# A scan and a gated FFN on one core: the second sequence's decays by matmul, its norm roots kept on chip, and a new order of steps

## The chip, the cores and the metric

The kernel runs on one core of a Trainium2 chip. Five engines work beside each other, each with its own queue that it works off in order: TensorE (PE, with its weight loads shown as PEld), VectorE (DVE), ScalarE (ACT), GpSimd (POOL) and SyncE (SP), which here issues nearly all DMAs. The metric is the device time of one execution in microseconds, as a median over runs. A profiled execution shows every instruction; its span goes from the first to the last instruction.

## The reference

Two blocks follow each other. The first is a state-space scan over 4 sequences with 8 heads, 768 positions, head size 32 and state size 16:

```python
for c in range(nc):                       # chunks of 32
    cum = np.cumsum(log_a[:, :, sl], axis=-1)
    L = np.exp(cum[:, :, :, None] - cum[:, :, None, :]) * causal
    y_intra = ((Cc @ Bc.T) * L) @ xc      # per batch and head
    y_inter = (Cc @ state) * np.exp(cum)[..., None]
    y[:, :, sl] = y_intra + y_inter
    state = decay_full * state + sum_j(B_j x_j * decay_from_j)
```

Its output, as 3072 tokens of 256 numbers, goes through an FFN (d_ff = 1536):

```python
rms = np.sqrt(np.mean(x * x, axis=-1, keepdims=True) + 1e-06)
xn = x / rms * rms_g
return (silu(xn @ w_gate) * (xn @ w_val)) @ w_out
```

## The kernel before

**Sequences.** The scan of a sequence b is cut into six chunks of 128 positions, taken in three pairs (p = 3b, 3b+1, 3b+2). The first two pairs of sequence 0 work on whole chunks, all other pairs on half chunks of 64. For a pair the kernel loads B, C (`bc`) and x, transposes B and C on PE (`turn`, copied out by `T` and `Tt`, and with a decay by `Td`), forms the new states (`A` on PE, `S` on DVE), the products of C and B (`g`), multiplies them by the decay table L (`L`, `L.0`, `L.1.3` and so on, on DVE), and forms the outputs (`y`). A group of A or g products holds both banks of PSUM that single tiles share.

**The decay table L** is made in one of two ways. Sequence 0 sums logs on PE: `log4` takes logs on ACT, `r` multiplies them with a triangular matrix, `parts` splits the result into three bfloat16 parts (`three_parts`), `mask` writes a mask of -2^100 into a pair of banks through an identity (line 445), `sums` adds the row and column sums with small matmuls (lines 459 and 466), and `exp` (line 474) takes the exponential on ACT. Sequences 1 to 3 instead store the sums of logs to DRAM (`rowout`, line 1158), read each row back spread over 64 partitions (`spread`, line 480, two DMAs a chunk), subtract the token's own sum on DVE (`sub`, line 486), take Exp on ACT and put zeros above the diagonal on POOL (`ex`, lines 492 and 494).

**The norm.** `sq` squares y on ACT and adds two halves on POOL, `ms` averages over channels by a matmul with 1/256, `rs` takes (mean + eps)^-1/2 as Exp(-0.5 Ln), and `xn` multiplies it in (line 840). Sequence 0 has the mean on all 128 partitions and uses the roots at once, in a piece of 512 tokens and one of 256 (`ms.0.1`, `rs.0.1`, `xn.0.1`). Sequences 1 to 3 keep the means in four groups of 32 partitions, store the roots to DRAM (line 821) and read them back spread, in four DMAs (`rb`, line 826).

**The FFN.** The weights arrive as 64-bit numbers and are turned into float32 by `pow` (three passes on ACT), `man` and `wt` (DVE). The first half of d_ff for sequence 0 runs early in plain form (`early`, `gate`, `silu`, `hid`, then `late`, `lsilu`, `lhid` for the last 256 tokens; lines 885, 858, 866). After that come stages s0 to s7: sequences 0 to 3 with the first half of the hidden units (s0 has only the output product), then 0 to 3 with the second half. A stage uses products of combined operands: `V` and `U` are combinations on DVE or POOL (a p behind the name means POOL), `P` the gate and value products (line 980), `take` and `C` move and combine them, `silu` and `hid` form the hidden units, `s`, `s2` to `s4` combine these, and `O` are the output products (line 1067).

**The order.** All queues are filled from one written list of about 1,660 steps, in its order. A step reads `0:kind.numbers`, `b1:kind.numbers` or `s1:kind.numbers`, and `/0` to `/2` names the pair of banks of a product in the first part. In front of an activation whose function isn't in the loaded table, the program gets a table load; steps named `table`, `exps` and `set` load one ahead of time.

Of the kernel before, what the change touches and what calls it, by code (L numbers as in the profile page):

```python
# [20 lines left out]
def kernel(  # L21
# [71 lines left out]
    st = {}  # L93

# [230 lines left out]
    def logs_again(g, n):  # L325
        b, c = divmod(g, NC)
        nc.scalar.activation(
            out=la4[g // 4][:, g % 4:g % 4 + n],
            in_=la0[:, c:c + n, b * NH:(b + 1) * NH].unsqueeze(2).to_broadcast([P, n, 4, NH]),
            func=AF.Ln)  # L330

    def minus_mid():
# [5 lines left out]
        "set": lambda: nc.scalar.preload_act_table_set("natural_log_exp_and_others"),  # L338
# [62 lines left out]
    def other_decays():  # L401
        nc.scalar.activation(out=d_sb, in_=ps.pop("d"), func=AF.Exp)
# [87 lines left out]
    def exponential(g):  # L490
        L = pair_tile(g)
        nc.scalar.activation(out=L, in_=L, func=AF.Exp)  # L492
# [300 lines left out]

    def norm_sums(b, third=None):

        if b == 0:
# [12 lines left out]
    def norm_roots(b, third=None):  # L809
        n = TB // 4  # L810
        if third:
            ps["r third"] = r = scan.tile([P, 256], FP32, tag="rest", name="r3", bufs=1)
        elif b == 0:
            ps["r", b] = r = hold.tile([P, 512], FP32, tag="sq2", name="r", bufs=1)
        else:
            r = scan.tile([P, n], FP32, tag="r_sb", name="r4", bufs=2)
        nc.scalar.activation(out=r, in_=ps.pop(("m", b, third)), func=AF.Ln, bias=eps)
        nc.scalar.activation(out=r, in_=r, func=AF.Exp, scale=-0.5)
        if b:
# [50 lines left out]
    def silu_late(f):  # L870
        us["late", f] = hold.tile([P, 256], FP32, tag="u", name="u", bufs=2)
        nc.scalar.activation(out=us["late", f], in_=ps["late", f][:, 0:256], func=AF.Silu)
# [25 lines left out]
    def silu_of(f):  # L898
        if f not in us:
            us[f] = hold.tile([P, 512], FP32, tag="b2", name="u", bufs=NB2)  # L900
            nc.scalar.activation(out=us[f], in_=ps["gv", f][:, 0], func=AF.Silu)
        else:
            nc.scalar.activation(out=us[f], in_=us[f], func=AF.Silu)
# [96 lines left out]
    def silu_gv(n, c, t):  # L1000
# [3 lines left out]
        else:  # L1004
            src = cs[c, n, t]
            u = src[:, half[0]]
        nc.scalar.activation(out=u, in_=src[:, half[0]], func=AF.Silu)  # L1007
# [153 lines left out]
    def row_decays(k):  # L1161
        c = 2 * k
        r_sb = scan.tile([P, P], FP32, tag="r_sb", name="e_sb", bufs=2)
        nc.scalar.activation(out=r_sb, in_=ps["row", k][:, 1], func=AF.Exp)
# [15 lines left out]
    def by_vector(out, in_, scale):  # L1180
# [32 lines left out]
        "table": lambda k: ac.preload_act_table(AF.Silu), "switch": switch,  # L1213
        "exps": lambda: ac.preload_act_table_set("natural_log_exp_and_others"),
# [29 lines left out]
    for name, fn in (("U", combine_u), ("V", combine_v), ("join", joined_gv), ("hid", hide_gv),  # L1244
                     ("two", combine_wo), ("s", combine_h), ("s3", difference_h), ("s2", second_h),
                     ("s4", fourth_h)):
        kinds[name], kinds[name + "p"] = on(dv, fn), on(pl, fn)
    scan_kinds = {
        "turn": of_pair(turn), "T": of_pair(lambda p: turned(p, ac.copy)),
# [10 lines left out]
        "table": lambda b: ac.preload_act_table(AF.Silu),  # L1260
        "exps": lambda b: ac.preload_act_table_set("natural_log_exp_and_others"),
# [3 lines left out]
        0:never 0:after 0:mid 0:fetch.0 0:upto2 0:mids 0:ident16 0:idle.7 0:fetch.1 0:whole16  # L1265
        0:mask.0.0/0 0:whole 0:hmask 0:tmask 0:part 0:gcol 0:part2 0:sel 0:mask.1.1/2 0:after2 0:aT
        0:kinks 0:la0 0:mask.0.1/1 0:log4.0.4 0:fetch.5 0:r.0 0:eps 0:parts.0 0:log 0:d 0:log4.4.2
        0:dx 0:c*2 0:cx 0:scale.0 0:log4.6.2 0:turn.0.1 0:bc.2 0:T.0.1 0:Tt.0.0.1 0:sums.0.1
        0:Tt.0.1.1 0:exp.0.1 0:turn.0.0 0:Tt.0.1.0 0:T.0.0 0:last.0 0:Tl.0 0:cc 0:fetch.3 0:pow.1
        0:sums.0.0 0:A.0 0:sums.1.1 0:man.0 0:fetch.2 0:Tt.0.0.0 0:exp.0.0 0:g.0.1/1 0:x.2 0:fetch.6  # L1270
        0:S.0 0:turn.1.1 0:T.1.1 0:Tt.1.1.1 0:fetch.4 0:middles b1:exps b1:bc.2 0:Tt.1.0.1
        0:turn.1.0 0:Tt.1.1.0 0:T.1.0 0:g.0.0/0 0:man.1 0:tok 0:L.0.1 0:Tt.1.0.0 0:mask.1.0/1
        0:scale.1 0:pow.0 0:man.5 0:tokout 0:row.1 0:rowout.1 0:sums.1.0 0:rowe.1 0:fetch.7
        0:exp.1.1 0:L.0.0 0:last.1 0:man.3 0:wt.0 0:r.1 0:man.2 0:parts.1 0:exp.1.0 0:dT.2 0:g.1.0/2
        0:L.1.0 0:y.0/1 0:Tl.1 0:fetch.11 0:pow.3 0:wt.3 0:g.1.1/0 0:L.1.1 0:A.1 0:S.1 0:wt.1
        0:y.1/2 0:row.0 0:pow.2 0:wt.2 0:sq.0 0:scale.2 0:pow.5 0:turn.2 0:never16 0:yt.0
# [7 lines left out]
        0:L1.2.2 0:L1.2.3 s0:U.1.0 0:L.2.0 0:silu.1 0:hid.1 b1:x.2 0:man.11 0:gate.5/0 0:silu.5  # L1284
        0:hid.5 b1:scale.1 0:fetch.10 0:y.2/2 0:sq.2 b1:bc.0 0:yt.2 b1:scale.0 s0:U.0.0 0:man.10
        0:fetch.9 b1:scale.2 0:man.9 0:ms.0.1 b1:table 0:rs.0.1 0:xn.0.1 0:gate.4/1 b1:dT.1 b1:A.0
        0:silu.4 b2:table b1:x.1 b1:spread.4 b1:spread.5 b1:sub.5 b1:A.1 b1:A.2 0:hid.4 0:ydone.0
        0:ydone.1 0:switch.1 0:pow.10 0:switch.0 0:late.3 0:lsilu.3 b1:S.0 b1:S.1 0:pow.9 b1:S.2
        0:fetch.13 0:late.1 0:lsilu.1 b1:turn.1 b1:Td.1 0:lhid.1 b1:turn.0 b1:Td.0 0:fetch.14
        0:late.0 b1:T.1 b1:Tt.1.1 b1:sub.4 b1:T.0 b1:Tt.0.0 b2:dT.1 b1:Tt.0.1 b1:dT.2 b1:Tt.1.0  # L1290
        0:wt.8 0:wt.9 s0:U.0.3 s0:Up.0.1 b2:bc.1 0:wt.11 b1:ex.4 b1:g.0 b1:L.0.3 s0:U.1.13 0:lhid.3
        b1:L.0.2 b1:turn.2 b1:ex.5 b1:T.2 b1:Td.2 b1:Tt.2.0 0:late.2 b1:L.0 s0:U.1.8 b1:Tt.2.1
        b1:g.1 b1:L.1 0:lsilu.2 b1:L.1.3 0:lsilu.0 b1:L.1.2 b1:y.0.0 b1:y.0.1 s0:U.1.14 b1:y.0.2
        b1:y.1.0 0:lhid.2 0:pow.13 0:lhid.0 0:late.4 0:pow.14 0:fetch.12 0:lsilu.4 s0:s.1 0:pow.12
        s0:Up.0.4 0:wt.10 b2:bc.2 b2:scale.1 s0:Up.1.22 s0:Up.1.3 b2:bc.0 s0:s.0 s0:two.0 0:man.12
        b2:scale.0 b1:y.1.1 b1:y.1.2 b1:y.2.0 b1:y.2.1 b1:y.2.2 0:late.5 b2:x.1 b2:spread.0
        b2:spread.3 b1:sq b2:spread.1 s0:two.1 b1:yt 0:man.13 s0:O.5.0 s0:two.2 0:wt.13 0:wt.12
        s0:O.1.0 s0:U.0.13 b2:spread.2 s0:two.3 b2:x.0 0:lhid.4 0:lsilu.5 b1:ms b1:rs s0:O.1.1
        s0:s3.0 s0:O.4.0 0:lhid.5 s0:s.2 s0:O.1.2 s0:Otake.1 s0:s2.0 0:man.14 b2:scale.2 0:wt.14
        s0:s3.1 s0:O.5.1 s0:s2.1 s0:O.5.2 s0:s2.2 s0:O.4.1 b2:sub.0 s0:O.6.0 s0:s4.0 s0:O.2.0  # L1300
        b2:sub.2 b2:sub.1 s0:O.2.1 s0:U.0.14 s0:O.6.1 s0:O.6.2 s0:s4.1 s0:s3.2 0:fetch.15 s0:O.4.2
        s0:s4.2 b1:rb b1:xn s1:Vp.12 s1:V.0 s0:O.2.2 s0:Oadd.11 s1:Vp.14 b2:x.2 s1:V.1 s0:Otake.6
        s0:O.7.0 s0:O.7.1 s0:O.7.2 s0:Otake.7 s0:Oadd.22 s1:P.13.1 s1:take.13.1 0:pow.15 b2:A.0
        b2:A.1 s1:V.7 s1:V.4 s1:Vp.11 s1:V.8 b2:A.2 s1:P.13.0 s1:Vp.10 s0:O.3.0 b2:spread.4 s0:O.3.1
        s0:O.3.2 b2:ex.0 b2:S.0 b2:S.1 s1:take.13.0 s1:P.11.1 0:fetch.18 b2:sub.3 0:man.15
        s0:Oadd.12 s1:take.11.1 s1:P.11.0 s1:take.11.0 s1:P.4.1 b2:spread.5 b2:sub.5 b2:ex.2 s1:Vp.6
        b2:dT.0 b2:S.2 s1:Vp.3 s1:Vp.9 b2:ex.1 b2:ex.3 s1:P.14.0 s1:take.14.0 s1:P.4.0 s0:Oadd.21
# [183 lines left out]
```

## Time and profile before

| what | us |
|---|---|
| median of 3 runs (434.02 to 437.09) | 434.12 |
| the profiled execution | 435.05 |
| its span, first to last instruction | 433.3 |
| first product of s1 starts (s1:P.13.1) | 111.01 |
| first product of s2 starts (s2:P.13.0) | 167.82 |
| first product of s3 starts (s3:P.13.1) | 219.16 |
| mean granted clock of PE | 0.966 |
| table loads on ACT, each | 1.28 |

Times in the profile count from the start of the span. A row of waits gives an engine and line, what released it, the total, how often, and the longest. A row of the chain gives the start, the time spent, and what the chain went through. A row of the timeline gives start and length, engine, line, operation, what it writes and reads, sizes and how many were merged.

### The profile page before, as it was taken

What the parts mean: (1) busy time and instruction counts of PE and PEld (TensorE: products, weight loads), DVE (VectorE), ACT (ScalarE), POOL (GpSimd) and SP (SyncE); (2) the same over time, 40 slices, a digit from 0 to 9 for tenths busy, and PEclk for the clock granted to TensorE, in tenths of its full rate; (3) what the DMA queues carried; (4) which work ended last, traced back from release to release, by engine and by line L of the source; (5) the groups of instructions that cost most, each with busy time, mean ns of one, the idle gap of its engine ahead of it and who ended that gap; (6) DMA issues with size and microseconds to landing.
All of it is one profiled execution on the core that took longest, in us unless ns stands there. A gap on an engine that the chain in (4) does not pass through costs nothing.

```text
span 433.3 us, 9717 instructions
## 1 busy us (share of the span) xinstructions
PE 402.3 (93%) x3865; PEld 338.1 (78%) x3865; DVE 322.1 (74%) x659; ACT 220.4 (51%) x425; POOL 162.8 (38%) x198
## 2 busy tenths in 40 slices
PE   8889787899798698999999999999999999999996
PEld 5566345579686588887888889898998999998895
DVE  6698878697887678985885796579477737865793
ACT  3788759692399574795624433344134323322310
POOL 3113600520486050293462463637231425442330
PEclk9699798899899989999999999999999999999999
DMA  9784974869419658030450010000102110201112
GB/s 113 174 204 161 184 148 126 140 134 219 116 39 107 194 143 166 26 135 3 129 210 2 0 74 2 1 39 36 37 1 72 39 38 0 75 36 38 36 46 101
DMA packets 96756, 38.37 MB, mean 89 GB/s; under 512 B 77608, under 2 KB 86696, under 8 KB 96712
## 3 DMA queue, kind: packets, MB, share of 16 engines
q1 hardware_dynamic: 92552, 37.50, 36.1%
q10 hardware_dynamic: 4160, 0.26, 0.7%
q8 instruction: 30, 0.49, 0.5%
q14 instruction: 14, 0.11, 0.1%
HBM read 28.54 MB, written 9.21 MB: 87 GB/s over the span
## 4 chain that ended last, share of the span: by engine, by line
PE 69%; ACT 11%; DMA 7%; DVE 5%; issue 3%; SPq 2%; POOL 1%; DVEq 0%; POOLq 0%; ACTq 0%
PE gate L980 33%; PE o L1067 21%; PE val L980 7%; PE y L723 3%; DMA r<-roots 2%; PE g L587 1%; PE gate L858 1%; DMA L<-rowd 1%; ACT p L985 1%; DMA roots<-r 1%; DMA rowd<-r_sb 1%; ACT L1260 1%; DMA wr<-in_moe_w_val_dram 1%; SPq L110 1%; DVE L L627 1%
## 5 line engine op out<-in xcount | busy, mean ns | idle before, releaser
L980 PE MATMUL gate<-V,u 128*128 128x256 f32 x336 | 84.9, 387 | 0.0
L980 PEld LDWEIGHTS gate<-V,u 128*128 128x128 f32 x336 | 61.0, 191 | 9.8 <-ACT p L985 0.7
L1007 ACT ACTIVATE p<-p 128x256 f32<-128x256 f32 x70 | 27.7, 412 | 47.7 <-DVE p L998 47.5
L980 PE MATMUL gate<-xn,u 128*128 128x256 f32 x168 | 44.2, 397 | 5.2 <-DVE xn L840 4.8
L985 ACT COPY p<-gate 128x512 f32<-128x512 f32 x42 | 24.3, 588 | 39.6 <-PE gate L980 36.4
L980 PE MATMUL gate<-V,wgv 128*128 128x256 f32 x168 | 42.6, 384 | 0.5 <-DVE c L998 0.5
L998 DVE TENSOR_TENSOR p<-gate,p 128x512 f32<-128x512 f32 x42 | 28.8, 687 | 16.4 <-PE gate L980 16.1
L980 PEld LDWEIGHTS gate<-xn,u 128*128 128x128 f32 x168 | 31.3, 198 | 11.1 <-DVE xn L840 3.7
L1067 PE MATMUL o<-wo,h 128*128 128x128 f32 x288 | 38.1, 277 | 0.3 <-DVE h L1013 0.3
L1067 PEld LDWEIGHTS o<-wo,h 128*128 128x128 f32 x288 | 36.5, 192 | 2.0 <-DVE h L1013 0.5
L1067 PE MATMUL o<-two,h 128*128 128x128 f32 x288 | 37.3, 275 | 0.0
L1067 PEld LDWEIGHTS o<-two,h 128*128 128x128 f32 x288 | 35.8, 192 | 1.2 <-DVE v L1098 0.2
L1067 PE MATMUL o<-two,s 128*128 128x128 f32 x288 | 36.1, 276 | 0.7 <-ACT xn L790 0.7
L985 ACT COPY p<-val 128x512 f32<-128x512 f32 x42 | 24.2, 584 | 24.1 <-PE val L980 20.7
L1067 PEld LDWEIGHTS o<-two,s 128*128 128x128 f32 x288 | 34.9, 192 | 1.8 <-ACT xn L790 1.1
L980 PEld LDWEIGHTS gate<-V,wgv 128*128 128x128 f32 x168 | 29.9, 190 | 5.6 <-DVE c L998 1.1
L494 POOL TENSOR_SCALAR_AFFINE_SELECT L<-L 64x512 f32<-64x512 f32 x36 | 26.8, 744 | 19.8 <-ACT L L492 18.2
L1013 POOL TENSOR_TENSOR h<-p 128x256 f32<-128x256 f32 x26 | 19.9, 772 | 36.2 <-ACT p L1007 35.3
L1007 ACT ACTIVATE c<-c 128x256 f32<-128x256 f32 x42 | 16.9, 414 | 30.8 <-DVE c L998 30.6
L980 PE MATMUL val<-V,u 128*128 128x256 f32 x112 | 28.5, 380 | 0.0
L998 DVE TENSOR_TENSOR p<-p,gate 128x512 f32<-128x512 f32 x28 | 18.9, 684 | 11.3 <-PE gate L980 8.6
L1013 POOL TENSOR_TENSOR h<-c 128x256 f32<-128x256 f32 x17 | 12.8, 759 | 35.2 <-ACT c L1007 35.2
(215 smaller groups left out, 812.8 us busy)
## 6 DMA issues: line engine op xcount, KB each, us to landing
L<-rowd SPq DMA_DIRECT2D x36, 128.0 KB, 3.4
xr<-in_x_dram SPq DMA_DIRECT2D x24, 128.0 KB, 4.4
wr<-in_moe_w_out_dram SPq DMA_DIRECT2D x6, 512.0 KB
part<-ob SPq DMA_DIRECT2D x8, 384.0 KB, 2.3
before<-part SPq DMA_DIRECT2D x8, 384.0 KB, 3.6
out_dram<-ob SPq DMA_DIRECT2D x8, 384.0 KB
wr<-in_moe_w_val_dram SPq DMA_DIRECT2D x5, 512.0 KB, 4.1
wr<-in_moe_w_gate_dram SPq DMA_DIRECT2D x5, 512.0 KB, 5.4
```

Source lines behind the costliest of these rows:

```text
L110: queue.dma_start(out=st[p]["x"][:, i], in_=x[b, :, sl, :].rearrange("h s n -> s h n"))
L494: nc.gpsimd.affine_select(out=L[r], in_=L[r], pattern=[[0, NH], [1, HC]], compare_op=ALU.is_ge, fill=0.0, base=0, channel_multiplier=-1)
L587: nc.tensor.matmul(out=g[u, P * i:P * i + P].rearrange("p (t m) -> p t m", t=2), lhsT=T[r, i, 0, u], rhs=T[r, i, 1:3, u], start=(first and ...
L627: nc.vector.tensor_tensor(out=L, in0=g.rearrange("p q (i m) -> p q i m", i=2), in1=L, op=ALU.mult)
L723: nc.tensor.matmul(out=y[2 * k + u][rows, (2 * n + i) * HC:(2 * n + i + 1) * HC], start=(k, u, rows.start) not in opened, stop=True, skip_ ...
L858: nc.tensor.matmul(out=gv[:, k], lhsT=w[:, t, fs], rhs=xns[0][:, t, 0:512], start=(t == 0), stop=(t == 1))
L980: nc.tensor.matmul(out=dst[:, half[w]], lhsT=lhsT[:, w], rhs=rhs, start=(k in (13, 14) and w == 0), stop=True, skip_group_check=True)
L985: nc.scalar.copy(out=v, in_=(Xs if chain[k] == "X" else Zs)[n, t])
L998: nc.vector.tensor_tensor(out=o, in0=in0, in1=in1, op=ALU.subtract)
L1007: nc.scalar.activation(out=u, in_=src[:, half[0]], func=AF.Silu)
L1013: engine.tensor_tensor(out=hidden_tile(n, f // 2)[:, f % 2, c % 10 - 1], in0=u, in1=src[:, half[1]], op=ALU.mult)
L1067: nc.tensor.matmul(out=o[:, t * P:(t + 1) * P], lhsT=lhsT[:, t], rhs=rhs, start=(opens and t == 0), stop=True, skip_group_check=True)
```

## The change

Sequence 1 makes its decay table as sequence 0 does: the steps `mask`, `sums` and `exp` exist for its three pairs, with the pair of banks 2, and six `spread`, `sub` and `ex` steps leave the list. For that a third group of log sums is formed (`log4.8.4`, `r.2`, `parts.2`). Sequence 1's roots are made as sequence 0's are, in two pieces on all partitions, and its `rb` step leaves the list. Table loads are made by a helper that remembers the loaded table. The list is in another order from its beginning up to the first product of s3; behind that it is the same.

```diff
+    loaded = [None]
+
+    def table(name):
+
+        if loaded[0] != name:
+            loaded[0] = name
+            if name == "silu":
+                nc.scalar.preload_act_table(AF.Silu)
+            else:
+                nc.scalar.preload_act_table_set("natural_log_exp_and_others")
...
     def logs_again(g, n):
         b, c = divmod(g, NC)
+        if g // 4 == len(la4):
+            la4.append(scan.tile([P, 4, 4, NH], FP32, tag="r_sb", name="la4", bufs=2))
+        table("exp")
         nc.scalar.activation(
...
+        table("exp")
         nc.scalar.activation(out=L.rearrange("p i h m -> p i (h m)"), in_=e, func=AF.Exp)
...
+    WIDE = (0, 1)
+
     def norm_sums(b, third=None):
 
-        if b == 0:
+        if b in WIDE:
             tk = slice(512, TB) if third else slice(0, 512)
...
-        if third:
+        if third and b == 0:
             ps["r third"] = r = scan.tile([P, 256], FP32, tag="rest", name="r3", bufs=1)
         elif b == 0:
             ps["r", b] = r = hold.tile([P, 512], FP32, tag="sq2", name="r", bufs=1)
+        elif b in WIDE:
+            if not third:
+                ps["r", b] = hold.tile([P, TB], FP32, tag="sq2", name="r", bufs=1)
+            r = ps["r", b][:, 512:TB] if third else ps["r", b][:, 0:512]
         else:
             r = scan.tile([P, n], FP32, tag="r_sb", name="r4", bufs=2)
+        table("exp")
         nc.scalar.activation(out=r, in_=ps.pop(("m", b, third)), func=AF.Ln, bias=eps)
+        table("exp")
         nc.scalar.activation(out=r, in_=r, func=AF.Exp, scale=-0.5)
-        if b:
+        if b not in WIDE:
             roots[b] = dram.tile([4, 32, n], FP32, name="roots%d" % b)
...
+    def start_decays_of(p):
+        ps["e", p] = e = pair_of_banks("e", 2)
+        mask(p, e)
+
     scan_kinds = {
+        "mask": of_pair(start_decays_of), "sums": of_pair(lambda p: sums(p, 0, ps["e", p])),
+        "exp": of_pair(lambda p: decay(p, 0, ps.pop(("e", p)))),
...
-        "table": lambda b: ac.preload_act_table(AF.Silu),
-        "exps": lambda b: ac.preload_act_table_set("natural_log_exp_and_others"),
+        "table": lambda b: table("silu"),
+        "exps": lambda b: table("exp"),
...
+        0:scale.2 0:wt.4 b1:x.1 0:T.2 0:ms.0 0:Td.2 0:man.6 0:rs.0 0:xn.0 b1:mask.1 b1:sums.1
+        b1:exp.1 0:pow.5 0:early.1.0/1 0:early.0.1 0:norm.0 0:early.1.1 0:Tt.2.1 0:tok 0:norm.1
+        0:Tt.2.0 b1:mask.0 0:tokout 0:A.2 0:S.2 0:pow.7 b1:sums.0 0:U b1:exp.0 0:gg.2/1 0:L1.2.3
+        0:pow.10 0:wt.5 0:gate.2/0 b1:bc.1 0:wt.6 0:L.2.0 0:L1.2.2 0:man.10 0:pow.8 0:man.7 0:y.2/2
...
+        s0:Up.0.3 0:hid.0 b1:A.0 b1:A.1 b1:dT.2 0:silu.5 0:hid.5 b1:A.2 b1:S.0 s0:Up.0.13 b1:mask.2
+        b1:sums.2 b1:exp.2 b1:S.1 0:ydone.1 0:ydone.0 0:switch.1 0:switch.0 b1:S.2 b2:bc.1 0:late.2
+        0:pow.11 b1:table s0:U.1.0 s0:Up.1.3 b1:g.0 b1:L.0.3 b1:L.0 b1:turn.2 b1:T.2 0:fetch.13
...
+        0:lsilu.5 b2:table s0:O.4.0 b1:ms b1:rs b1:ms.1 s0:O.5.1 b1:rs.1 0:lhid.5 s0:s.2 b2:scale.0
+        s0:twop.2 s0:s2.1 b1:xn 0:man.15 s0:O.2.0 s0:O.2.1 s0:O.2.2 s0:s2p.0 b2:spread.1 s0:O.5.2
+        s1:V.6 s0:U.1.14 0:fetch.14 s0:O.1.0 s0:O.1.1 s0:O.1.2 s0:Otake.1 s1:V.1 s1:Vp.7 s1:P.13.1
```

The helper is called in the same way ahead of the other activations (`exponential`, `row_decays`, `silu_of`, `silu_late`, `silu_gv` and the rest); no line of those functions changes otherwise. In the list before, the same places read:

```diff
-        0:early.0.0/0 0:sq.1 0:rowe.0 0:rowout.0 0:ms.0 0:early.1.0/1 0:wt.5 0:man.6 b1:spread.0
-        b1:spread.2 0:pow.4 0:pow.6 0:T.2 0:man.4 0:rs.0 0:yt.1 0:pow.7 0:man.7 b1:spread.1
-        0:mask.2/2 0:wt.6 0:wt.4 0:early.0.1 0:sums.2 0:xn.0 0:norm.0 0:U 0:wt.7 s0:U.0.8 s0:Up.0.22
-        s0:Up.0.5 b1:sub.0 s0:U.1.5 s0:Up.0.12 b1:dT.0 b1:sub.1 0:exp.2 0:early.1.1 b1:sub.2
-        0:pow.11 b1:ex.0 0:Td.2 s0:Up.1.12 b1:ex.1 s0:Up.0.7 b1:ex.2 b1:spread.3 b1:sub.3 0:Tt.2.0
-        s0:Up.1.7 0:norm.1 0:gate.2/0 b1:ex.3 0:silu.2 0:fetch.8 0:man.8 0:hid.2 s0:U.1.4 0:Tt.2.1
-        0:gate.3/2 0:A.2 0:S.2 0:pow.8 0:silu.3 0:hid.3 0:silu.0 b1:bc.1 b1:x.0 0:hid.0 0:gg.2/1
...
-        s0:s3.0 s0:O.4.0 0:lhid.5 s0:s.2 s0:O.1.2 s0:Otake.1 s0:s2.0 0:man.14 b2:scale.2 0:wt.14
...
-        s0:s4.2 b1:rb b1:xn s1:Vp.12 s1:V.0 s0:O.2.2 s0:Oadd.11 s1:Vp.14 b2:x.2 s1:V.1 s0:Otake.6
```

More of the change, by code (lines that the diff above doesn't have):

```diff
@@ L1006, in silu_gv @@
             u = src[:, half[0]]
+        table("silu")
         nc.scalar.activation(out=u, in_=src[:, half[0]], func=AF.Silu)
@@ L1264 @@
         0:warm 0:a 0:set 0:bc.0 0:ident 0:bc.1 0:ones 0:x.0 0:zeros 0:mean 0:head 0:upto 0:x.1
[L1265 to L1275, printed above, removed]
@@ L1288 @@
[L1288 to L1293, printed above, removed]
@@ L1371 @@
-        s3:P.7.1 s3:silu.13.1 s3:hid.13.1 s3:join.1 s3:C.12.1 s3:sp.0 s3:silu.12.1 s3:hid.12.1
-        s3:s.1 s3:hidp.21.1 s3:O.1.2 s3:Otake.1 s4:U.3.2 s4:P.11.0 s3:O.5.0 s3:O.4.0 s4:take.11.0
+        0:never 0:after 0:mid 0:fetch.0 0:upto2 0:mids 0:ident16 0:idle.7 0:fetch.3 0:whole 0:eps
+        0:kinks 0:fetch.4 0:fetch.2 0:whole16 0:mask.1.1/2 0:hmask 0:after2 0:mask.0.1/1 0:tmask
+        0:bc.2 0:aT 0:fetch.5 0:la0 0:log4.0.4 0:log4.8.4 0:log4.4.2 0:mask.0.0/0 0:gcol 0:never16
+        0:part 0:part2 0:turn.0.1 0:T.0.1 0:Tt.0.0.1 0:r.0 0:Tt.0.1.1 0:fetch.1 0:parts.0 0:log
@@ L1373 @@
+        s3:silu.13.1 s3:hid.13.1 s3:join.1 s3:C.12.1 s3:sp.0 s3:silu.12.1 s3:hid.12.1 s3:s.1
+        s3:hidp.21.1 s3:O.1.2 s3:Otake.1 s4:U.3.2 s4:P.11.0 s3:O.5.0 s3:O.4.0 s4:take.11.0
         s3:hidp.33.1 s4:P.13.1 s4:U.2.0 s3:O.2.1 s3:sp.2 s3:s3.0 s3:O.4.1 s3:s2.0 s3:s3p.2 s3:O.5.1
```

184 lines of the change are left out of this document (101 added, 83 removed).

## The prediction

> **What bounds the kernel now.** I read the page's busy shares first, then a table by three stretches (up to the first product of stage s1 at 111, up to the first product of s3 at 219.16, the rest), then what TensorE (PE) waited for, then the chain that ended last around the two longest waits, then the granted clock behind them, and last the rows that price what is added.
>
> ```profile
> PE 402.3 (93%) x3865; PEld 338.1 (78%) x3865; DVE 322.1 (74%) x659; ACT 220.4 (51%) x425; POOL 162.8 (38%) x198
> ```
>
> PE is the bound by its share, but the stretches differ.
>
> ```profile
> 0.00:111.00 111.00, 92.12 (x1157) 63.31 (x1157) 87.23 (x207) 76.36 (x132) 26.70 (x43) 0.91 0.79 159
> 111.00:219.16 108.16, 101.01 (x1419) 84.79 (x1420) 87.01 (x179) 75.31 (x138) 49.81 (x59) 0.97 0.45 110
> 219.16:433.30 214.14, 209.16 (x1292) 189.99 (x1290) 147.87 (x275) 68.70 (x155) 86.31 (x96) 1.00 0.12 41
> ```
>
> The columns are length, PE, weight loads, VectorE (DVE), ScalarE (ACT), GpSimd (POOL), PE clock, DMA share, GB/s. In the last stretch PE is full at full clock, and the change leaves its order alone: it stays 214.1. In the first stretch PE idles 18.9 us and runs at 0.91 of its clock while DVE (79%) and ACT (69%) are busy but not full either: that stretch is bound by chains between the engines. There the change acts.
>
> ```profile
> PE gate L980 <- DVE xn L840: 4.8, 2, 3.5
> PE y L723 <- issue: 3.3, 2, 2.0
> PE A_ps L653 <- ACT T L1178: 3.1, 1, 3.1
> PE tp L530 <- DVE A L667: 2.4, 1, 2.4
> PE ms L800 <- POOL sq L772: 1.6, 1, 1.6
> ```
>
> The reader is to see three waits of 3.5, 3.1 and 2.4 us: before the first product of s1, before A.2 at 50.1, and before b1's first transposes at 72.0. The chain of waits tells where the first two come from:
>
> ```profile
> 32.41 3.98 DMA rowd<-r_sb
> ...
> 39.55 4.86 DMA L<-rowd
> ...
> 47.80 1.28 ACT L901
> ...
> 50.11 0.47 PE A_ps L653 x16
> ```
>
> ```profile
> 95.47 1.28 ACT L817
> 97.21 1.28 ACT L818
> 98.95 4.51 DMA roots<-r
> 104.86 4.02 DMA r<-roots
> 109.01 1.96 DVE xn L840 x2
> ```
>
> The first piece is b1's decay table, which goes out to DRAM and comes back spread; DVE, then ACT, stand in their queues behind it, and PE's A.2 behind ACT. The second is b1's norm roots, out and back again. Behind each of the three waits the clock is halved (the clock's column: 0.50):
>
> ```profile
> 49.19:56.02 6.83, 5.91 (x53) 3.13 (x54) 6.75 (x15) 4.48 (x8) 3.25 (x5) 0.50 1.08 172
> 73.08:79.91 6.83, 5.74 (x73) 4.13 (x72) 3.70 (x9) 4.87 (x11) 3.11 (x5) 0.50 0.65 118
> 110.63:114.04 3.41, 3.03 (x79) 2.20 (x85) 3.15 (x8) 0.92 (x2) 2.04 (x3) 0.50 0.85 260
> ```
>
> A step `late` takes 3.78 us in the second of these (at 73.91) against 1.86 to 1.99 outside, so half of the PE busy time in such a window is lost.
>
> **The change part by part**, in us of the profiled span of 433.3. That execution took 435.05, so 1.75 lies around its span; the median of the three runs is 434.12, 0.93 below it.
>
> (a) Norm roots of b1 stay on chip. Two wide mean products replace four narrow ones, a second pair Ln and Exp is added, and the store and the four reads leave SP's queue. From the end of the squares' sum (POOL, 95.97) to the start of xn (109.01) it now takes 13.04. Without the DMA: products 1.0 (ms.0, 32.45 to 33.47), Ln and Exp at 512 wide 1.35 (rs.0, 35.16 to 36.51), at 256 wide 0.9 (0.47 + 0.42): 3.3, with the table load beside POOL's sum. xn comes 9.7 earlier. PE's cover between mean products and P.13.1 falls from fourteen O steps to nine (some 6 us at 0.67), still more than 3.3 + xn's 1.96. The 3.54 wait goes, and half of the 3.03 behind it: -5.0.
>
> (b) b1's decays on TensorE. Six spreads (twelve DMAs of about 0.6 on SP), six subtracts (0.69 on DVE), six Exps of 512 (0.63 on ACT) and twelve selects (0.74 on POOL) go; three mask and sums steps on PE and three Exps of 1024 (1.0 on ACT) come. In the changed order turn.2's copies stand ahead of the first silu, with no spread ahead of them on DVE or ACT. So A.2's 3.12 goes and half of the 5.91: -6.1. What is late next there is ACT's powers, four groups of 2.26, which PE's early, gate and sums steps cover. The price on PE, by pair 2's own steps:
>
> ```profile
> 35.03 0.59 PE L445 MATMUL e<-never,ident 128*128 128x512 bf16 x2
> 37.29 0.44 PE L459 MATMUL e<-row,sel 32*64 32x64 bf16 x32
> 37.56 0.39 PE L466 MATMUL e<-sel,row 32*64 32x512 bf16 x4
> ```
>
> Start to the next start: 0.44 + 0.59 = 1.03 a pair, 3.1 for three. The wide mean products add 1.0 + 0.7 - 0.53 = 1.2. Together +4.3 if all of it lies on the path; 0 if it only fills idle time. I take +4.3, as PE is the fullest engine of both stretches.
>
> (c) b1's states and group products. The gaps from 69.59 to 84.94 sum to 2.44 + 0.81 + 0.92 + 0.20 + 0.84 = 5.2. In the changed order silu.5, hid.5 and three S steps (0.6 + 0.69 + 4.1 = 5.4) stand between gate.5 and the two banks that g.0 needs, while PE has A, mask, sums and late.2 (0.7 + 1.0 + 1.9 = 3.6); that leaves 1.8 idle, and about 1.0 more until L.0.3 frees a bank for turn.2: 2.8, so -2.4. The half clock behind (5.74, half of it 2.9) followed a gap of 2.44; gaps of 2.01 and more were each followed by one, 1.59 was not, and the first window (at 15.05) stands behind one of only 1.36; at 1.8 I take half, -1.4; ends 0 and -2.9.
>
> The Trainium skill, "TensorE: Matmul & The Clock Gate", in "Why this matters for your kernels", allows idle gaps up to about 3 us before the clock falls. By that this term would be 0, as 2.44 would have cost nothing, and the sum 1.4 higher; the trace has a halved window behind 2.44 and behind 2.01, so the measurement decides.
>
> (d) Table loads. Up to s1 the trace has 12, the changed program 7; from there to s3 13 become 15. At 1.28 each that is -6.4 and +2.6 on ACT. Those on the chain are within (a) and (c); the others lie under ACT's own idle time (31% and 30%). I take 0; ends -3 and +2.6.
>
> The Trainium skill, "ScalarE: Activation LUTs", in "What ACT_TABLE_LOAD costs", adds a drain of some 1.38 us to each. Here the load at 47.80 ends at 49.08 and the next activation starts at 49.09, so no drain shows; by the page five loads fewer would free 13.3 on ACT, not 6.4, and the sum would stay, since ACT's time is covered.
>
> (e) The new order. A check by sums: every instruction that stands ahead of s1:P.13.1, at its form's median in this trace (starts to next starts), gives PE 78.5, DVE 85.0, ACT 78.9 before and 76.2, 75.1, 70.6 after; ahead of s3:P.13.1 170.0, 164.9, 157.2 before and 173.9, 160.2, 154.4 after. So between the two PE gets 97.7 instead of 91.5. At DVE's old density the first stretch takes 111 x 75.1/85.0 = 98.1; at PE's the second 108.16 x 97.7/91.5 = 115.5. That ends at 213.6, 5.6 earlier. Waits of the new order are not in the trace; the nearest row is the 2.01 stall of y L723, and I take one such: +2.0; ends 0 and two waits like A.2's with half clocks, 12.
>
> Sum: -5.0 - 6.1 + 4.3 - 2.4 - 1.4 + 0 + 2.0 = -8.6; by density -5.6. I take -7.1 between them: span 426.2, execution 427.95, by the median's offset 427.0.
>
> **The rivals.** Two waits return: the ways freed are filled, but small waits eat (e) and (c). Then (a) + (b) - 6 or more: -5 - 6.1 + 4.3 + 6 is about -1, and 433. For it speaks that the order is wholly new over half the span; against it that each engine's sum ahead of s1 falls.
>
> Slower: the pair of banks 2 is the mechanism. In the changed order b1's decays, y.2, gate.3, and b1's group products pass through it in turn, and each Exp of 1024 that frees it stands behind powers on ACT, with all of PE behind the next user. If ACT is late, each of three passes waits a power group and an Exp, 2.27 + 1.0 = 3.3, and pays a halved window, 3.4 at most: up to 6.7 x 3 = 20 against the 8.6 + 2.0 gained without waits: +9, 443; with two such passes about 437. It decides only where ACT runs late by more than its lead in the sums of (e), 4.6 at y.2 and 3.7 at g.0. Against it: ACT's sum ahead of y.2 (37.1) is no larger than PE's (37.5).
>
> Larger gain: added PE work only fills idle time and (c) pays in full and no wait is new: -5.0 - 6.1 - 5.2 - 2.9 = -19.2, 415.
>
> **How the numbers follow.** Forecast 0.55 (418 to 430), absorbed 0.22, slower 0.16, larger gain 0.07. About 1% (4.3 us) is what a measurement of this kernel can tell from no change. The forecast's upper end and the absorbed case share the middle: faster by over 1% 0.60, within 1% 0.24, slower 0.16. The range runs from 418 (most of the larger gain left out) to 438 (the absorbed case and the edge of the slower one).
>
> **What would show it.** In the changed profile: no 3.5 us wait at the first P of s1, which starts near 98 to 102; no wait over 2 us at A.2; no halved clock near those places; DMA r<-roots with eight reads, not twelve; s3's first product near 212; the last stretch still 214. Wrong would be: PE waits at y.2, gate.3 or g.0 for an Exp L491, or halved windows at new places before 111.

## The result, and the profile after

The changed kernel takes 414.85 us (median of 4 runs, 413.87 to 415.58) against 434.07 (4 runs, 432.86 to 437.09): ratio 0.955, interval 0.949 to 0.960. The forecast was 427.0 with a range from 418 to 438: the gain is 19.2 us where 7.1 were forecast, and the time lies below the range. The profiled execution took 415.26, its span 413.6.

The page's first lines of the changed kernel:

```profile
PE 398.6 (96%) x3977; PEld 335.5 (81%) x3977; DVE 318.8 (77%) x650; ACT 216.9 (52%) x422; POOL 160.8 (39%) x193
```

The three stretches again (length, PE, weight loads, DVE, ACT, POOL, PE clock, DMA share, GB/s), cut at the first product of s1 (89.16) and of s3 (199.37):

```profile
0.00:89.16 89.16, 83.83 (x1222) 56.34 (x1222) 78.64 (x190) 67.04 (x121) 21.59 (x35) 1.00 0.81 157
89.16:199.37 110.21, 105.52 (x1468) 89.13 (x1467) 91.18 (x185) 81.25 (x146) 54.81 (x63) 0.98 0.50 115
199.37:413.60 214.23, 209.28 (x1291) 190.01 (x1290) 148.98 (x277) 68.57 (x155) 84.36 (x95) 1.00 0.14 45
```

The first stretch is 21.8 us shorter (89.16 instead of 111.00), the second 2.1 longer, the third the same. In the first PE idles 5.3 us instead of 18.9, and no halved window shows in its clock. What PE waits for in the whole span:

```profile
PE gate L1009 <- issue: 2.5, 1, 2.5
PE o L1097 <- DVE s L1064: 1.2, 1, 1.2
PE idle L324 <- DVE warm L351: 1.1, 1, 1.1
PE y L741 <- issue: 1.0, 1, 1.0
PE tp L548 <- DVE L L639: 0.8, 1, 0.8
```

None of the three long waits shown of before is left. The chain of work around b1's norm, where the round trip through DRAM stood:

```profile
78.71 0.17 ACT sq L788
...
80.29 0.70 ACT xn L808
...
81.03 1.60 PE o L1097 x12
82.64 1.29 PE ms L820 x4
83.93 5.39 PE o L1097 x48
89.32 0.87 PE gate L1009 x4
```

PE goes from the mean products through output products into s1 without a stop; xn (DVE, from 85.8) is ready before it is asked for. The last squares were summed at 82.17, so the 13.04 us from there to xn have become 3.6.

**Where the 19.7 us of span went.** From the trace I take three sums up to the start of the last xn ahead of s3: the time that PE idled; half of PE's busy time in windows where the clock is 0.50 (the time lost to the clock, an estimate: large products take twice as long there, `late` 3.78 us instead of 1.86 to 1.99, while 16 of the smallest at A.2 took 0.47 us in such a window and 0.35 in b_tables, outside of one); and what is left of PE's busy time (the work at full clock). The remainder of the span is 215.3 to 216.5 in every run.

| | before | after | difference | the forecast's terms |
|---|---|---|---|---|
| idle | 26.0 | 10.0 | -16.0 | -3.5 - 3.1 - 2.4 + 2.0 = -7.0 |
| lost to the clock | 12.1 | 1.7 | -10.4 | -1.5 - 3.0 - 1.4 = -5.9 |
| work | 179.5 | 186.5 | +7.0 | +4.3 |
| sum | 217.6 | 198.2 | -19.4 | -8.6 |

The added work was forecast too small, the gain in idle time at less than half of its size and the clock's at 0.57 of it.

Two limits of this table. First, the trace's record of the clock begins only with the first full clock, at 4.82 us in the profile of before and at 9.25 in that of the changed kernel. Until then the same two products take nearly twice as long; the first row is from before, behind that point, the second from the changed kernel, ahead of it:

```profile
5.97 0.67 PE L370 MATMUL r_ps<-mids,la 128*128 128x256 f32 x2 [0.30 <-issue]
7.23 1.06 PE L384 MATMUL r_ps<-mids,la 128*128 128x256 f32 x2
```

Counted as half clock too, this start moves 1.9 us (before) and 3.7 us (after) from the work to the clock: the clock's difference is then -8.6 and the work's +5.1, close to the forecast's 4.3. In the other profiles the record begins between 3.95 and 9.95 us. Second, each row is one profile, and the clock differs from run to run: the profile of before has a mean of 0.966, its 64 runs beside the experiments 0.965 to 0.988 with a median of 0.976, and the four of the changed kernel 0.994 each. So the clock's part of the gain stands at the upper end here.

### The profile page after: what moved, and what is told of

It is laid out like the page before. It is cut to its first block, busy times and chain, and to the rows that moved or that the text cites. A ratio compares the mean times of both kernels' runs of the same rounds, so it can differ in the third digit from the quotient of the medians.

```text
span 413.6 us, 9867 instructions
## 1 busy us (share of the span) xinstructions
PE 398.6 (96%) x3977; PEld 335.5 (81%) x3977; DVE 318.8 (77%) x650; ACT 216.9 (52%) x422; POOL 160.8 (39%) x193
## 4 chain that ended last, share of the span: by engine, by line
PE 74%; DVE 12%; ACT 5%; DMA 3%; issue 3%; POOL 1%; SPq 0%; DVEq 0%; ACTq 0%; POOLq 0%
PE gate L1009 34%; PE o L1097 24%; PE val L1009 7%; PE y L741 3%; PE late L892 2%; DMA dT<-rowe 1%; DVE L L645 1%; PE g L605 1%; DVE m L202 1%; ACT L104 1%; DVE wgv L210 1%; DMA L<-rowd 1%; DMA cr<-in_C_dram 1%; PE e L461 1%; ACT T L1209 1%
## 5 line engine op out<-in xcount | busy, mean ns | idle before, releaser
L1043 POOL TENSOR_TENSOR h<-p 128x256 f32<-128x256 f32 x27 | 21.7, 808 | 46.9 <-ACT p L1037 45.5
L1027 DVE TENSOR_TENSOR p<-p,gate 128x512 f32<-128x512 f32 x28 | 19.2, 684 | 11.1 <-PE gate L1009 10.0
L1027 DVE TENSOR_TENSOR c<-p,gate 128x512 f32<-128x512 f32 x28 | 19.2, 685 | 11.0 <-PE gate L1009 9.7
```

The costliest lines, as they stand in the source:

```text
L1027: nc.vector.tensor_tensor(out=o, in0=in0, in1=in1, op=ALU.subtract)
L1043: engine.tensor_tensor(out=hidden_tile(n, f // 2)[:, f % 2, c % 10 - 1], in0=u, in1=src[:, half[1]], op=ALU.mult)
```

## The experiments

Two theories went into the first runs. P: the three new parts (roots on the chip, decays on PE, loads on a change) carry the gain, and the order only gives them room. O: the new order carries it. The runs took place on several chips, so each kernel is compared with the kernel before on its own chip (medians there 432.1 to 434.1); the ratio is the safer number, and a difference of two medians from different chips is a rough one. Idle, clock and work are the three sums of above from each run's profile, the start not counted as lost.

| run | order | decays on PE | roots on chip | helper | median | ratio (interval) | idle | clock | work |
|---|---|---|---|---|---|---|---|---|---|
| before | old | no | no | no | 434.07 | 1 | 26.0 | 12.1 | 179.5 |
| b_tables | old | no | no | yes | 429.27 | 0.996 (0.991 to 1.001) | 20.6 | 13.0 | 178.4 |
| b_wide | old | no | yes | yes | 426.77 | 0.990 (0.986 to 0.994) | 20.8 | 8.2 | 180.2 |
| b_sums | old | yes | no | yes | 429.68 | 0.995 (0.991 to 0.999) | 17.1 | 11.9 | 183.2 |
| b_all | old | yes | yes | yes | 427.73 | 0.989 (0.985 to 0.993) | 17.4 | 10.2 | 184.1 |
| a_order | new | no | no | no | 438.86 | 1.016 (1.010 to 1.023) | 29.1 | 10.2 | 181.3 |
| a_order_tables | new | no | no | yes | 433.56 | 1.004 (1.000 to 1.008) | 24.7 | 9.5 | 180.6 |
| a_spread | new | no | yes | yes | 426.85 | 0.990 (0.982 to 0.997) | 20.4 | 7.2 | 181.2 |
| a_roots | new | yes | no | yes | 419.47 | 0.972 (0.965 to 0.980) | 14.2 | 3.4 | 185.3 |
| a_loads | new | yes | yes | no | 427.38 | 0.987 (0.983 to 0.991) | 19.1 | 3.4 | 186.3 |
| changed kernel | new | yes | yes | yes | 414.85 | 0.955 (0.949 to 0.960) | 10.0 | 1.7 | 186.5 |

**The parts in the old order (b_tables, b_wide, b_sums, b_all).** The code is that of the changed kernel, the list that of before with these edits:

```diff
 b_tables
-    WIDE = (0, 1)
+    WIDE = (0,)
 b_wide
-b1:ms b1:rs ... b1:rb b1:xn
+b1:ms b1:rs b1:ms.1 b1:rs.1 ... b1:xn
 b_sums (WIDE = (0,) too; b1's six spread, sub and ex leave the list)
+0:log4.8.4 ... 0:r.2 0:parts.2 0:row.1 ... 0:early.1.1 b1:mask.1 b1:sums.1 ... b1:exp.1
+0:gate.2/0 b1:mask.0 b1:sums.0 b1:exp.0 ... b1:A.2 b1:mask.2 b1:sums.2 ... b1:exp.2
 b_all: b_wide and b_sums
```

> The old order and the old parts, only with table loads made by the helper that remembers the table. Theory T (loads on ACT lie on the chain from 60 to 68, where four stand in a row): 3 to 6 us faster than before, 428 to 431. Rival C (ACT's loads are covered): within 2 us, 432 to 436.

> The old order with the roots of sequence 1 on chip in two pieces, and the table helper. By the prediction's term (a): the 3.54 us wait before s1's first product and its halved window go, 5 us less than the run with the helper alone. Rival: PE only does its output products of s0 earlier and waits for DVE's sums instead: within 1.5 us of it.

> The old order with sequence 1's decays on TensorE in place of spread, subtract, Exp and select, and the table helper. By the prediction's term (b): the wait at A.2 and its halved window go (6.1 us), added PE work 3.1 us: 3 us less than the run with the helper alone. Theory P gives more, 6 us or over, since added PE work fills idle time. Rival: the pair of banks 2 makes PE wait for Exps: no gain or a loss.

> The old order with all three new parts put in by hand where their counterparts stood: mask, sums and Exp for sequence 1, roots in two pieces on chip, table loads only on a change. Theory P: 418 to 425, the waits at A.2 and at the first product of s1 gone with their halved windows. Rival O: 429 to 437, PE's gaps reappear under other releasers.

All three parts together give 1.1%, some 4.6 us; that is between the two theories. The helper alone, b_tables, takes 0.4% with an interval that reaches no change. The roots in b_wide give 2.5 us more than that (0.6% by the ratios), half of the 5 expected: in its profile the wait at s1 is gone, but the one for xn at s2 has grown from 1.45 to 2.73 us. The decays alone give nothing beyond the helper (429.68 against 429.27 on the same chip), the rival's outcome, though the wait at A.2 is gone: idle falls by 3.5 and the clock's loss by 1.1, and the work rises by 4.8. In b_all PE waits for new things:

```profile
PE y L741 <- issue: 3.0, 1, 3.0
PE gate L1009 <- DVE xn L866: 1.8, 1, 1.8
PE g L605 <- ACT L L491: 1.8, 1, 1.8
PE ms L820 <- POOL sq L790: 1.8, 1, 1.8
PE g L598 <- DVE T L1212: 1.3, 1, 1.3
PE gate L884 <- ACT L L491: 1.1, 1, 1.1
```

The two rows of L491 are the Exps of 1024 that free the pair of banks 2: the mechanism of the forecast's slower rival, at 2.9 us in all, in the old order and not in the new one.

**The order alone (a_order, a_order_tables).** The changed kernel with b1's decays and roots made as before; a_order also has the explicit load steps of this list in place of the helper, which a_order_tables keeps. `tok` and `tokout`, which `sub` needs, stand further ahead in both.

```diff
-    WIDE = (0, 1)
+    WIDE = (0,)
-0:log4.8.4 ... 0:r.2 ... 0:parts.2 ... b1:mask.1 b1:sums.1 b1:exp.1 ... b1:ms.1 ... b1:rs.1
+0:fetch.8 b1:spread.2 b1:spread.3 b1:spread.0 b1:spread.1 ... b1:sub.2 b1:sub.3 b1:ex.2 b1:ex.3 ... b1:rb b1:xn
...
 a_order only: def table(name)
-        if loaded[0] != name:
+        return
```

> The new order with the old parts: sequence 1's decays come again through DRAM (spread, subtract, Exp, select), its norm roots too, and table loads are placed as before. Spreads stand behind the store of the sums, subtracts and Exps where the changed order had its Exps. Theory P (the two DRAM round trips held PE up, and the idle gaps behind them halved its clock): the waits are back, 428 to 438, PE idle ahead of s3 over 18 us, at least three halved windows. Rival O (the new order as such packs PE fuller, the parts matter little): 414 to 421.

> The new order with the old parts (decays of b1 spread and subtracted, norm roots of b1 through DRAM), but with the helper that loads a table on a change only. The same with the explicit loads took 438.9. Theory: the new order was slow there through the loads, which are worth as much here as with the new parts (12.5): 426.4; the sum of the two parts undone one by one in the changed kernel gives 414.9 + 4.6 + 12.0 = 431.5; so 426 to 432, about the 429.3 of the old order with the helper. Rival: the order itself is worse without the parts, whatever the loads: 436 to 439.

So the order alone is worth nothing: 0.4% slower than before with the helper, 1.6% without. The 438.86 of a_order lies just above the range of P, and the 433.56 of a_order_tables between the ranges of its two theories. O falls. P falls as well, since the same parts give 1.1% in the old order, and in the new one what separates a_order from the changed kernel, 24.0 us by the medians and 6.2% by the ratios. What PE waits for in a_order_tables:

```profile
PE A_ps L671 <- ACT T L1209: 4.2, 1, 4.2
PE y L741 <- issue: 4.0, 3, 1.6
PE gate L1009 <- DVE xn L866: 3.8, 2, 3.6
PE g L605 <- DVE A L685: 2.8, 1, 2.8
PE A_ps L671 <- DMA xr<-in_x_dram: 2.4, 2, 1.7
PE tp L548 <- DVE r_sb L1187: 1.6, 1, 1.6
```

The first, third and fourth are the three long waits of before, at A.2, at s1 and at b1's products. The new order moves work forward, but with the old parts it meets the same round trips. In the fifth b1's states wait for a late x: its loads stand in SP's queue behind two spread steps and start at 59.02, against 47.07 in a_roots, which has no spread of b1.

**One part undone in the new order (a_roots, a_spread).** Edits as above, the roots alone and the decays alone (a_spread also drops the third group of log sums and moves `tok` and `tokout` as above).

```diff
 a_roots
-    WIDE = (0, 1)
+    WIDE = (0,)
-b1:ms b1:rs b1:ms.1 ... b1:rs.1 ... b1:xn
+b1:ms b1:rs ... b1:rb b1:xn
 a_spread
-b1:mask.1 b1:sums.1 b1:exp.1 ... b1:mask.0 b1:sums.0 b1:exp.0 ... b1:mask.2 b1:sums.2 b1:exp.2
+b1:spread.2 b1:spread.3 b1:spread.0 b1:spread.1 ... b1:sub.2 b1:sub.3 b1:ex.2 b1:ex.3 ...
```

> The changed kernel with sequence 1's norm roots again through DRAM; the read back stands right ahead of xn. By P: xn comes some 9 us later, PE has about 6 us of output products to cover it, so a gap of 3 to 6 us and a halved window of 3.4 us behind it: 419 to 424. By O: under 417.

> The changed kernel with sequence 1's decays again through DRAM, placed as in the run with the new order alone. By P: DVE and ACT stand behind the spreads, PE gaps of 3 us or more near 35 to 50 with halved windows, less 3 us of mask and sums: 420 to 428. By O: under 418.

Both lie in the ranges of P. Without the roots on the chip the time rises by 4.6 us by the medians (by the ratios 1.8%), without the decays by 12.0 (3.5%). The chain of a_roots shows the round trip back in its place:

```profile
83.77 1.63 DMA roots<-r
...
86.77 2.18 DMA r<-roots
...
89.08 1.96 DVE xn L866 x2
91.04 0.04 issue
91.09 1.13 PE gate L1009 x4
```

PE waits 3.1 us there and has half its clock from 92.2 to 95.6: idle +4.2, clock +1.7, less 1.2 of work is 4.7, near the 4.6 of the medians (most of the 1.2 is an earlier full clock in this profile, from 6.89 us instead of 9.25, and not the mean products). The decays are the larger part: against a_order_tables, a_roots has them on PE and nothing else, and there idle falls by 10.5 and the clock's loss by 6.1 for 4.7 of work. The first, fourth, fifth and sixth wait of a_order_tables, 11.0 us together, are all gone in it. In the old order the same edit (b_sums against b_tables) gave 3.5 and 1.1 for 4.8. The price is the same in both orders; the yield is not. Within one order the two parts nearly add up: by the ratios roots and decays give 0.6 and 0.1%, together 0.7%, in the old order, and 1.4 and 3.2%, together 4.9%, in the new one. It is the order that changes what a part is worth.

**The loads (a_loads, a_loads_root).** a_loads is the changed kernel with the explicit load steps of its list only, and the loads that the program then adds by itself; a_loads_root adds one load of the joint table ahead of each root.

```diff
 a_loads: def table(name)
-        if loaded[0] != name:
+        return
...
-        "table": lambda b: table("silu"),
+        "table": lambda b: preload("silu"),
 a_loads_root, besides
-        table("exp")
+        preload("exp")
         nc.scalar.activation(out=r, in_=ps.pop(("m", b, third)), func=AF.Ln, bias=eps)
```

> The changed kernel with the explicit table loads of the kernel before instead of the helper that loads a table on a change only. Loads lie on ScalarE, which is busy 217 of 414 us. If the order and the parts on TensorE carry the whole gain, the time stays at that of the changed kernel, 414.9 (414 to 417). Rival: the loads are a part of the gain, since the chain of b1 (square, root, normalisation) passes through ScalarE: then a load inside that chain moves its end by one load, 1.3 us, at each place, and the time is 416 to 420.

> The changed kernel with explicit loads (427.4), and one load of the joint table of logarithm and exponential ahead of each norm root. In the run with the explicit loads each root took two loads, logarithm and exponential one each (89.33 and 91.33, 93.27 and 95.06 in b1; 53.38 and 55.17 in b0). Theory: these lie in the chain that TensorE waits for at the start of b1's products; one load of 1.28 fewer per root then gives 2.6 in b1 and 1.3 in b0: 423.5 (422 to 425). Rival: what counts are the loads ahead of the decays and band products (60.69 to 70.83, with idle TensorE of 1.43 and 1.47 and a halved clock behind them): 426 to 428.

A surprise, outside both ranges: without the helper 12.5 us are lost (3.3% by the ratios), two thirds of the whole gain. ACT's rows around b1's roots in a_loads:

```profile
88.04 1.28 ACT L104 ACT_TABLE_LOAD   x1
89.33 1.28 ACT L844 ACT_TABLE_LOAD   x1
90.62 0.69 ACT L844 ACTIVATE r<-ms,eps 128x512 f32<-128x512 f32 x1
91.33 1.28 ACT L846 ACT_TABLE_LOAD   x1
92.62 0.63 ACT L846 ACTIVATE r<-r 128x512 f32<-128x512 f32 x1
93.27 1.28 ACT L844 ACT_TABLE_LOAD   x1
94.56 0.47 ACT L844 ACTIVATE r<-ms,eps 128x256 f32<-128x256 f32 x1
95.06 1.28 ACT L846 ACT_TABLE_LOAD   x1
```

and in the changed kernel:

```profile
82.33 1.28 ACT L104 ACT_TABLE_LOAD   x1
83.62 0.69 ACT L842 ACTIVATE r<-ms,eps 128x512 f32<-128x512 f32 x1
84.34 0.63 ACT L844 ACTIVATE r<-r 128x512 f32<-128x512 f32 x1
84.88 0.46 ACT L842 ACTIVATE r<-ms,eps 128x256 f32<-128x256 f32 x1
85.37 0.42 ACT L844 ACTIVATE r<-r 128x256 f32<-128x256 f32 x1
```

Five loads against one in the same chain: a load step of the list brings the silu table at 88.04, which nothing uses, and then Ln and Exp fetch a table each, twice. PE waits 1.06 and 0.78 us for the two roots there, and 1.44 for xn. 15 loads stand ahead of s1's xn in a_loads, 7 in the changed kernel and 12 in before (33, 22 and 25 in all). a_loads_root, with 29, takes 420.60 (0.974, interval 0.970 to 0.979): the roots carry 6.8 of the 12.5 (1.3 of the 3.3% by the ratios), about half. The rest is in what remains (three loads ahead of b1's roots instead of one, and loads ahead of the decays and band products, behind which PE still waits 1.47 at 59.3). I had expected 3.9 from the roots, so the result lies outside both ranges of that run. The runs do not say what the 25 loads of before would cost in the new order: a_loads has 8 more than that, since the load steps that the new list kept do not fit it. So 12.5 us is the price of these 33 loads, and not what the change of loads brought against before.

**All roots on the chip (a_wide_all).**

```diff
-    WIDE = (0, 1)
+    WIDE = (0, 1, 2, 3)
-... b2:ms b2:rs ... b2:rb b2:xn ... b3:ms b3:rs ... b3:rb b3:xn
+... b2:ms b2:rs b2:ms.1 b2:rs.1 ... b2:xn ... b3:ms b3:rs b3:ms.1 b3:rs.1 ... b3:xn
```

> The changed kernel with the norm roots of all four blocks formed on the chip, not of b0 and b1 alone: the DRAM round trips of the roots of b2 and b3 go, and two small products on TensorE come in. Theory: the roots were worth their round trip only where TensorE had nothing queued behind them (the start of b1's products); those of b2 and b3 lie under the products of the block before, so that the time stays: 414 to 416. Rival: the starts of s2 and s3 wait for their round trips as s1 did, and each that goes gives 1 to 3.5 us: 408 to 413.

415.74 (ratio 0.959, interval 0.955 to 0.963): no gain over the changed kernel, as the theory had it. The round trips of b2 and b3 cost nothing that these runs can tell, that of b1 in a_roots 4.6 us by the medians.

**The clock by itself (b_filled, b_early, b_all_early).** Useless products on zeros fill idle time of PE: in b_filled ahead of A.2 (16), of b1's first transposes (20) and of s1's first product (30), in the kernel before; in b_early 11 of them in the idle time that before has at 12.0 us; in b_all_early the same 11 in b_all.

```diff
+    def fill(flat, n):
+        for k in range(n):
+            nc.tensor.matmul(out=flat, lhsT=warm[:, 0:P], rhs=warm, start=True, stop=True)
...
 b_filled
-0:gate.3/2 0:A.2
+0:gate.3/2 0:fill.1.16 0:A.2
-0:lsilu.1 b1:turn.1
+0:lsilu.1 0:fill.2.20 b1:turn.1
+            if (n, t) == (1, 1):
+                fill(Xs[n, t][:, 0:256], 30)
 b_early, b_all_early
-0:exp.0.0 0:g.0.1/1
+0:exp.0.0 0:fill.1.11 0:g.0.1/1
```

> The kernel before with idle time of PE filled by matmuls on zeros that nobody reads (16 ahead of A.2, 20 ahead of b1's first transposes, 30 ahead of s1's first product), into banks that stand free there. No wait is taken away. If the halved clock costs time of its own: the three windows behind these gaps go and the time falls by 3 to 7 us, 427 to 431. If the chains between the engines set the end whatever PE's clock: within 1.5 us of before.

> The kernel before, with 11 useless matmuls on zeros ahead of the second band product of the first sequence, in the idle time of 1.36 us at 12.0 us, and nothing else. Theory: that idle time is what the halved clock from 15.05 to 21.88 us follows, and the window costs half of TensorE's busy time in it, 3.1 us: time 429 to 430, and no window before 24 us; where the runs of before had the longer window (17.1 us, seen in three of its variants), 8. Rival: the window has another cause (all the idle time up to 15 us together, the loads of the start), stays where it is, and the time stays at 432 to 434.

> The old order with all three new parts (427.7 us, halved clock from 15.9 to 33.0 us, idle time of 1.26 us at 12.1) and the same 11 useless matmuls in that idle time. Theory: most of what the new order adds to the parts is that TensorE stays busy over the first 16 us; then the window of 17.1 us goes, worth some 8, and the time is 419 to 421, 5 above the changed kernel. Rival: the order's worth is in the gaps further on (1.8 at 60.8 and 76.1, 3.0 at 138.9, 1.8 at 159.7), and the window either stays or moves to the next gap: 425 to 428.

b_filled took 428.11 (0.991, interval 0.987 to 0.996), in the range of a halved clock that costs time of its own. In its profile the gaps at A.2 and at s1 are filled, with no window behind them; ahead of the transposes the 20 products ran too early, and the wait for DVE A stayed at 2.09 us with a window of 3.4 behind it. So a full PE at two of the three places, with no chain taken away, gives about 4 us. The early halved window grew to 17.1 us in that profile; it was not in the forecast's sum. It stands in the profiles of all six kernels with the old order and no filling at 12 us (6.8 us long in three, 17.1 in three), and in none with the new order. In b_all it covers nearly all of these two rows, from 15.95 to 33.01 (the clock is the third number from the end):

```profile
16.00:24.00 8.00, 8.00 (x34) 4.82 (x32) 5.48 (x13) 4.53 (x11) 0.00 (x0) 0.50 0.84 176
24.00:33.00 9.00, 9.00 (x112) 5.71 (x110) 6.60 (x16) 6.00 (x12) 0.73 (x1) 0.50 0.79 187
```

and in b_all_early it is gone:

```profile
16.00:24.00 8.00, 7.02 (x66) 4.45 (x68) 7.59 (x17) 5.93 (x15) 0.00 (x0) 1.00 0.82 208
24.00:33.00 9.00, 7.53 (x120) 5.30 (x110) 8.74 (x21) 8.31 (x15) 1.46 (x2) 1.00 0.88 206
```

A later start of the full clock (9.8 to 10.0 us in both runs with this filling) does not by itself explain it: in b_filled, unfilled at this place, the start is at 9.68 and the window stands. b_all_early took 424.05 (0.979, interval 0.975 to 0.984), 3.7 less than b_all: the filling pays there, less than the 7 to 9 expected. In b_early the window is gone from the profile as well, and the time is the same as before (433.63, ratio 1.002, interval 0.997 to 1.007), although all four of its runs have a higher clock (0.979 to 0.987) than all seven of before on that chip (0.968 to 0.976). Neither theory of that run had this. The rows of PE in b_early tell why:

```profile
46.37 0.32 PE L665 MATMUL A_ps<-xr,Bd 64*32 64x64 f32 x8
50.16 0.35 PE L665 MATMUL A_ps<-xr,Bd 64*32 64x64 f32 x16 [3.48 <-ACT T L1190]
```

A.2's wait is 3.48 instead of 3.12 us and ends at 50.16 instead of 50.11: the chain through b1's decays sets that time, whatever PE has won. In b_all (first row below) that chain is gone and A.2 waits for nothing, yet it starts at 54.10, later than in before, since PE itself is late; in b_all_early (second row) the gain passes through:

```profile
54.10 0.43 PE L671 MATMUL A_ps<-xr,Bd 64*32 64x64 f32 x24
50.64 0.43 PE L683 MATMUL A_ps<-xr,Bd 64*32 64x64 f32 x24
```

So up to A.2 the time of the old order was held by two things at once, PE's own idle time, clock and work and the chain outside PE, and taking away one uncovers the other. That the same holds further on is likely from the small yields, but no run shows it place by place.

## Why the prediction was wrong

- **(a), the roots: right.** Forecast -5.0, less 1.2 of work; undone in the changed kernel +4.6 by the medians (1.8% by the ratios), with a wait of 3.1 us and a halved window of 3.4 us at the same place.
- **(b), the decays: the cause right, the yield far too small; with (e) the step that failed most.** The price on PE is 4.7 to 4.8 us (with the start counted as lost, 4.9 in the new order and 4.0 in the old), not 3.1; the mask and sums steps take about what was said (from 58.35 to 59.48 for b1's third pair, 1.13 against 1.03), and the third group of log sums brings two more products of 0.41 (r_ps, six instead of four), which the forecast left out: 4.2 of the 4.7. The yield is 16.6 in the new order (10.5 idle, 6.1 clock) and 4.6 in the old one; forecast 6.1. The forecast priced A.2's wait and the window behind it. The same part also ends the waits of b1's group products (2.8 us, the place that (c) priced), of its states for a late x (2.4) and of sequence 0's transposes (1.6); 6.1 us of the clock's loss go with them. (b) and (c) together were 9.9 in the forecast.
- **(c), the group products: wrong by its size.** I left 2.8 us of the 5.2 of idle time and half of the window. In the changed kernel 0.8 is left (the transposes waiting for DVE L) and no window. Of the 2.8, the 1.8 ahead of g.0 did not come (it starts at 61.40 without a wait), and the 1.0 ahead of turn.2 came as 0.8. It comes with the decays: with the old decays in the new order (a_spread) the wait of 2.38 us for DVE A is back at 70.5, and half the clock from 74.0 to 80.8 behind it, as before had it. The Trainium skill, which the forecast weighed there ("TensorE: Matmul & The Clock Gate", "Why this matters for your kernels"), warns only of idle gaps over about 3 us; by that the window's part would have been 0, and this row, too, stands against it.
- **(d), the table loads: the reason wrong, the size open.** "I take 0; ends -3 and +2.6" because the loads lay under ACT's idle time. ACT is idle for half of the span, but loads inside the chain of a root are not covered by it: 29 loads instead of 33, the four fewer all at roots, are worth 6.8 us (a_loads_root). Nothing but the load's own time stands there: the load at 82.33 ends at 83.61, and the next activation starts at 83.62. Before has such a chain at b0's root as well: loads at 60.44, 61.73 and 63.51, the first (silu) used by nothing, where the changed kernel has one. What the helper brought against the loads of before is measured in the old order only, 0.4% with an interval that reaches no change, which does not contradict the 0; in the new order it is worth 5.3 us with the old parts (1.2% by the ratios) and 12.5 with the new ones, against loads that fit that list badly.
- **(e), the new order: failed.** "Waits of the new order ... one such: +2.0": instead of one more wait, some 7 us of idle time beyond the priced 9.0 went, and the early halved window at 15.05 too. The forecast named that window in (c) as evidence and credited no step with its end; the changed order keeps PE busy for 15.6 of the 16 us from 8 to 24, with no halved window. The order does not do the rest by itself: with the old parts it is 0.4% slower than before. What it does is to let the parts pay. And "at DVE's old density the first stretch takes 98.1": the density is what the change raises. DVE's sum of 75.1 fitted into 89.16 us (0.84, before 0.77), and the second stretch took 110.2, not 115.5. Taking the middle of the sum and of this estimate (-7.1) moved the forecast the wrong way.
- **The rivals.** The larger gain, "added PE work only fills idle time and (c) pays in full and no wait is new", gave 415 at a chance of 0.07; the number came, by another sum and so by luck: the work was paid for (7.0, or 5.1 with the start counted as lost), and more idle time and clock came back than that rival had. The slower one, the pair of banks 2, is real in the old order (2.9 us in b_all) and absent in the new.
- **The signs.** Right: no long wait at s1 or A.2, no halved clock near them, eight reads of the roots, a last stretch of 214.2. Wrong: s1 at 89.2 instead of 98 to 102, s3 at 199.4 instead of 212.

In one sum: all terms but the roots' (b, c, d, e and the decays' work) were forecast at -4.8; a_roots, which has all but the roots, stands 14.8 below before in the same sum (202.9 against 217.7). The failure common to (b), (c) and (e) is that each part was priced by the waits of the old order. Beside the helper, both parts together give 1.5 us in the old order (429.27 to 427.73, by the ratios 0.7%) and 18.7 in the new one (433.56 to 414.85, 4.9%). Still open: which moved steps make the room. b_all_early, the old order with all parts and the early filling, is 9.2 us behind the changed kernel, and its idle time is 8.8 longer, in rows such as two stops without a releaser (4.2), the mean products waiting for POOL (1.8), the group products for ACT (1.8) and xn at s2 (1.4); no run moved those one by one.

## What to carry to other kernels

- A stretch that two things hold at once, the bound engine's idle time and chains outside it, can't be priced wait by wait: removing one alone shows little (b_early, b_sums), removing both shows more than the sum (b_all_early here, and the changed kernel). Ask of each removed wait what else held that moment, and of a new order whether it is the condition under which the parts pay.
- Do not cover table loads by an engine's idle share. Count them inside each short chain that the bound engine waits for, and look for loads whose table nothing uses.
- An old density applied to new sums assumes that nothing changes but the amount of work; an edit made to remove waits changes the density.

## What the runs showed of the hardware

The halved clock is less regular than the profile of before suggested. Its windows (the last one of each profile, which runs past the end, aside) lasted 3.41, 6.83 or 17.07 us, that is one, two or five times 3.41; the longest in b_all followed an idle time of only 1.26 us at 12.1, after 1.1 at the very start. The same kernel has more or fewer of them from run to run (mean clock of before 0.965 to 0.988). In the changed kernel a stop of 2.49 us at 129.7 was followed by a window from 132.1 to 135.5; in a_wide_all a stop of 2.62 at 129.2 was followed by none, and in b_all_early two of 2.1 by none. So the length of one stop does not decide it, and a forecast that counts windows by it has an error of a few us. These stops belong to the releaser "issue": PE waits there for nothing that the profile shows, for 1 to 3 us in long runs of small products (y at L741 in the changed kernel's list) or one product behind them (the 2.49 and the 2.62, between two gate products), and no run here found their cause.
